# A gated recurrence and a highway layer on one core: a new order of all operations

## The chip, the cores and the metric

The kernel runs on one core of a Trainium2 chip. The metric is the device time of one execution in microseconds (us); lower is better. The engines are named as the profile names them: PE (TensorE matmul), PEld (TensorE weight load), DVE (VectorE), ACT (ScalarE), POOL (GpSimd) and SP (SyncE, which here only issues DMAs).

## What is computed

```python
# x, f_logit: (4, 6336, 256) float32;  lower_bound, b_t: (256);  w_h, w_t: (256, 256)
f = lower_bound + (1 - lower_bound) * sigmoid(f_logit)
for t in range(S):                       # separately for each of the 4 sequences
    h = f[:, t] * h + (1 - f[:, t]) * x[:, t]
    y[:, t] = h
H = relu(y @ w_h)
T = sigmoid(y @ w_t + b_t)
out = T * H + (1 - T) * y
```

The recurrence runs along the sequence, so it is one long chain over 6336 steps for each sequence; the highway layer behind it works on each token alone.

## The kernel before

The 25,344 tokens are cut into 28 units (list `units`, L42 on): two of 256 tokens, one of 512, 23 of 1024, one of 512 and one of 256. A unit holds 2, 4 or 8 blocks of 128 tokens. The 256 channels are two halves `h` of 128, and the recurrence is done with channels on partitions and tokens along the free axis. One tuple of `units` ends with a number, the split: of the product `e = d * t` of that unit, the elements below the split are done by POOL in pieces of 512, and the rest by DVE in one piece.

Every operation of the kernel is a token of one long string, `order`. The loop at the end of the kernel reads the tokens from left to right and calls `do_<letter>` for each; every instruction is pinned to that order on its engine (`pin`). `s12.1:0` is the scan of unit 12, half 1, into buffer 0 of its kind; a `v` behind the numbers puts the operation on DVE instead of its usual engine; `*5` puts five matmuls on zeros ahead of it. Thus the string settles the order on each engine, SP's queue of DMAs among them, and which buffer each tile takes. A tile that takes a buffer waits until the last reader of the tile before it is done.

What the letters do for unit `n`, with the line that the profile shows:

- `l`, `x`: DMA of the logits and of the inputs, 1 MB each for a full unit (L263, issued by SP; six buffers each). `w`: DMA of half an output unit (L394, SP).
- `u`: sigmoid of minus the logits for the whole unit (ACT, L275). `b`: `u * x` for two blocks (POOL, or DVE with `v`, L283).
- `i`: transposes of `u` for one half into PSUM (PE, L289). `f`: the gate of that half from them (ACT L300, or DVE with `v`, L298). `p`: transposes of `b` (PE, L309). `i` and `p` share two PSUM buffers.
- `s`: the scan of one half (DVE, L326).
- `z`, `g`: the two products with the weights (PE, L338 and L141). `t`: sigmoid of `z` (ACT, L351). `d`: the rest of the relu and the difference to y (DVE, L355). `E`, `e`: `d * t` on POOL in pieces, and on DVE (L360).
- `o`: adds `e` and the scaled y and transposes back (PE, L379 and L380). `c`: copy from PSUM (ACT L389, or DVE with `v`, L387). `z`, `g` and `o` share three PSUM buffers.
- Single words: `wh`, `wt` (weight DMAs), `pc`, `cc`, `dg`, `WH`, `WTa` (constants and scaled weights), `k` (matmuls on zeros).

`shared` adds one more dependence: the first POOL operation behind a DVE operation of kind `b`, `e`, `dg` or `WH` in the list waits for that DVE operation.

```python
        if not gpsimd:
            held[:] = [ins]
        elif held:
            tc.add_manual_dep(ins.ins, held.pop().ins.name, mybir.DependencyInfo(
```

Of the kernel before, what the change touches and what calls it, by code (L numbers as in the profile page):

```python
# [83 lines left out]
f7.0:1 c4.1:2 d6.0:0 p7.0:0 E5.0 i8.0:1 z6.1:0 s7.0 u10:1 z6.0:1 g6.1:2 b8.3 l12:5 f8.0:0 b8.1 E5.3 E5.2 w3.1 w4.1
i9.0:1 p8.0:0 b9.3 b9.2 d6.1 o5.1:2 s8.0:0 t6.1:0 t6.0 f9.0:2 g7.0:1 i9.1:1 E6.3:0 c5.1:3 p8.1:0 x10:4 E6.2 z7.0:0
l11:0 E6.1 d7.0:2 o5.0:2 f9.1:1 g7.1:1 u12:0 s8.1 c5.0:0 p9.1:1 d7.1 i10.1:0 t7.0:1 f10.1:0 z8.0:2 z7.1:1 b10.0:1
b10.1 g8.1:0 p9.0:0 t8.0:2 z8.1:2 t7.1 s9.1:2 d8.1:1 u11:2 g8.0:1 w5.1 i12.1:1 E6.0 t8.1 b10.2 s9.0 x11:5 b10.3
f12.1:3 o6.1:0 e7:2 x12:0 d8.0 o6.0:2 i11.1:1 w5.0 p10.1:0 b11.3:2 z9.0:1 c6.1:1 f11.1:1 e8:1 b12.3:0 i10.0:1 g9.0:0
l13:1 c6.0:2 s10.1:1 t9.0:0 b11.1 b11.0 l15:2 b12.0 z9.1:2 f10.0:2 p10.0:0 o7.1:1 w6.1 i11.0:1 t9.1 g9.1:2 c7.1:3
d9.0:0 s10.0 o7.0:1 d9.1 f11.0:0 b11.2 p11.0:0 w6.0 b12.2 u13:1 s11.0:3 E9.1:0 x13:1 z10.1:2 E9.0 c7.0:0 e9 t10.1:1  # L90
g10.1:0 w7.1 i13.1:1 d10.1:2 b12.1 p11.1:0 s11.1 u15:2 g10.0:2 E9.2 o9.1:1 o9.0:0 f13.1:2 x15:2 E8.0 l14:3 b13.0:1
i12.0:1 b13.2 c9.1:1 w7.0 b13.3 i15.1:0 z11.0:1 b15.1:2 f12.0:0 p12.0:1 d10.0 z10.0:2 c9.0:2 x14:3 t11.0:0 o8.0:0
f15.1v:1 t10.0 w9.0 p12.1:0 b13.1 o8.1:2 s12.0:2 g11.1:1 c8.0:3 s12.1 i13.0:1 u14:0 E10.0:2 z12.1:0 b15.0 w9.1 d11.1:0
p13.1:0 z11.1:1 f13.0:0 i14.1:1 c8.1:0 e10 b14.1:0 w8.0 s13.1:0 g11.0:2 b14.2 t12.1:2 t11.1 l16:4 z12.0:0 b14.3
f14.1:3 w8.1 b14.0 x16:4 g12.0:1 t12.0 i14.0:0 p13.0:1 f14.0:2 d11.0 o10.0:2 d12.0:1 o10.1:1 c10.0:2 s13.0 l17:5
g12.1:0 E11.2:0 E11.0 E11.1 i15.0:1 p14.1:0 d12.1 c10.1:1 u16:1 z13.0:2 g13.0:0 e12:1 t13.0:1 f15.0:0 s14.1:1 o11.0:1
c11.0:3 E11.3 z13.1:2 p14.0:1 b16.3:1 b15.2 t13.1 b15.3 i16.0:0 f16.0:3 o11.1:1 d13.0:2 b16.0 g13.1:2 i16.1:0 w10.1
s14.0 c11.1:0 w10.0 p15.1:1 l20:0 d13.1 u17:0 w11.0 x17:5 b16.1 E12.0 s15.1:3 f16.1:2 z14.1:1 z14.0:0 b16.2 g14.1:2
d14.1:0 p15.0:1 l19:1 w11.1 i17.1:0 t14.1:0 E13.2:2 E13.3 s15.0 o12.1:2 E13.1 t14.0 g14.0:0 l18:2 x19:0 x18:1 u20:2
o12.0:1 c12.1:1 w12.1 d14.0 E13.0 p16.0:1 z15.0:2 b17.1:0 l21:3 f17.1:1 b17.0 b17.3 c12.0:2 E14.2:0 p16.1:0 t15.0:2  # L100
b17.2 s16.0:2 o13.1:1 g15.0:0 E14.1 i17.0:1 u19:1 o13.0:2 s16.1 f17.0:0 d15.0:1 p17.0:0 s17.0:0 g16.0:0 c13.0:3
c13.1:0 p17.1:1 u18:0 z15.1:1 E14.0 z16.1:2 E14.3 d16.0:2 i19.1:0 s17.1 g16.1:0 t15.1 w12.0 w13.0 x21:3 g15.1:1 d15.1
f19.1:3 w13.1 i18.0:0 i20.0:1 b19.1:2 b19.3 t16.1:1 g17.0:2 x20:2 b18.2:1 f18.0:2 i18.1:0 o14.0:1 b18.0 d16.1 d17.0:0
b18.3 b18.1 e15:1 E15.1 g17.1:0 o14.1:2 d17.1 b19.2 E15.0 f20.0:0 f18.1:1 c14.0:1 p18.1:1 u21:0 z16.0:1 z17.0:0
s18.1:1 t16.0 p18.0:0 o15.1:1 t17.0:0 b19.0 s18.0 b21.2:0 o15.0:0 c14.1:2 p19.1:1 z17.1:2 c15.1:3 e16:2 E17.1:0
b20.1:1 c15.0:0 i19.0:0 z18.1:1 b20.0 b20.3 l22:4 t17.1 b20.2 w14.0 g18.0:0 f19.0:1 z18.0:2 w14.1 p19.0:0 s19.1:3
E17.3 i20.1:1 d18.0:1 w15.1 t18.1:2 t18.0 o16.1:1 E17.0 g18.1:2 o16.0:0 b21.1 s19.0 d18.1 f20.1:2 w15.0 p20.0:1
i21.1:0 l23:5 u22:1 b21.0 g19.1:2 c16.1:1 s20.0:2 f21.1:3 b21.3 E17.2 c16.0:2 g19.0:1 i21.0:0 d19.1:2 f21.0:1 i22.0:1
z19.1:0 p20.1:0 f22.0:0 o17.1:2 p21.1:1 d19.0 x22:4 z19.0:1 t19.1:1 s20.1 c17.1:3 o17.0:2 w16.1 u23:2 w16.0 l24:0
i23.1:0 E19.2:1 g20.1:0 e18:2 t19.0 z20.1:1 b22.0:2 f23.1:2 p21.0:0 s21.1:0 i22.1:1 c17.0:0 b22.2 E19.0 b22.3 d20.1:0  # L110
b22.1 s21.0 g20.0:0 o18.0:2 t20.1:0 f22.1:3 u24:0 o18.1:1 p22.1:0 p22.0:1 x23:5 w17.1 d20.0 E19.1 z20.0:0 c18.0:1
z21.1:2 c18.1:2 z21.0:1 s22.1:1 t20.0 i24.0:0 w17.0 s22.0 x24:1 E19.3 g21.1:0 b23.2:1 t21.1:2 f24.0:1 b23.3 t21.0
d21.1:1 b23.1 g21.0:2 i24.1:1 d21.0 l25:1 b23.0 w18.0 E21.2:0 f24.1:3 i23.0:0 o19.1:0 e20:2 g22.1:1 o19.0:2 f23.0:0
w18.1 c19.1:3 c19.0:0 b24.0:0 b24.2 x25:0 p23.1:1 b24.1 p23.0:0 z22.1:0 u25:1 d22.1:2 l27:2 o20.0:2 s23.1:3 o20.1:1
c20.0:1 i25.1:1 b24.3 c20.1:2 E21.3 s23.0 t22.1:1 g22.0:2 E21.0 z22.0:1 f25.1:2 b25.1:2 w19.1 b25.2 w19.0 p24.0:0
z23.1:0 b25.0 t22.0 d22.0 l26:3 g23.1:2 t23.1:0 b25.3 i25.0:1 z23.0:1 s24.0:2 w20.0 p24.1:0 f25.0:0 o21.0:0 w20.1
d23.1:0 p25.0:1 g23.0:2 s24.1 u27:2 E21.1 t23.0 g24.1:1 c21.0:3 x26:2 u26:0 o21.1:0 E22.1:1 E22.3 d23.0 E22.0 p25.1:0
x27:3 d24.1:1 o22.1:2 E22.2 b26.1:1 b26.0 z24.1:1 c21.1:0 s25.0:0 c22.1:1 E23.0:2 z24.0:0 o22.0:2 i26.1:1 t24.1:2
# [316 lines left out]
```

## Time and profile before

| what | value |
|---|---|
| time, median of 3 runs (range) | 210.58 us (210.58 to 211.62) |
| the profiled execution: its own time, its span | 210.7 us, 208.9 us |
| DVE busy | 195.6 us, 155 instructions |
| ACT busy | 193.6 us, 189 instructions |
| PE busy | 192.8 us, 1827 instructions |
| POOL busy | 173.4 us, 164 instructions |
| mean DMA rate over the span | 377 GB/s, 78.69 MB moved |
| granted TensorE clock | 0.996 |

The span is the stretch from the first to the last instruction or transfer of the profiled execution; its own time is 1.8 us longer. A busy engine is one with an instruction under way; matmuls overlap, so PE's busy share is not its load. A group's mean is the time of one instruction, and neighbours on one engine overlap by some 0.07 to 0.1 us.

### The profile page before, as it was taken

Reading aid. Unit: us, or ns where it says so; the run is one execution under the profiler, and the core shown is the slowest. Engines: PE = TensorE matmul, PEld = TensorE weight load, DVE = VectorE, ACT = ScalarE, POOL = GpSimd, SP = SyncE. Lnnn points to the kernel's source line nnn. Section 1 sums busy time; section 2 is a strip of 40 time slices with the busy share of each in tenths; the row PEclk is TensorE's granted clock in tenths of the full one; section 3 lists DMA queues with packets and bytes.
Section 4 is the critical chain, followed back from the end, with each engine's and each line's share of the span. In section 5 each row is a group of like instructions: output and inputs, shape, how many; then the busy total and the mean of one; then the engine's idle time right before and its main releaser. Section 6 shows DMA issues by size and latency. Waiting matters only on the chain.

```text
span 208.9 us, 4672 instructions
## 1 busy us (share of the span) xinstructions
PE 192.8 (92%) x1827; PEld 132.9 (64%) x1827; DVE 195.6 (94%) x155; ACT 193.6 (93%) x189; POOL 173.4 (83%) x164
## 2 busy tenths in 40 slices
...
GB/s 226 393 426 417 416 419 425 417 408 424 416 422 405 420 401 346 402 413 378 421 384 381 425 417 420 427 414 427 406 362 315 322 418 409 368 229 190 176 328 254
DMA packets 15982, 78.69 MB, mean 377 GB/s; under 512 B 1748, under 2 KB 2264, under 8 KB 10072
## 3 DMA queue, kind: packets, MB, share of 16 engines
...
q8 instruction: 14, 0.23, 0.4%
q14 instruction: 8, 0.07, 0.1%
q10 hardware_dynamic: 8, 0.00, 0.0%
...
## 4 chain that ended last, share of the span: by engine, by line
PE 44%; DVE 20%; DMA 13%; ACT 10%; issue 6%; POOL 4%; SPq 1%; DVEq 0%; ACTq 0%
DMA l<-in_f_logit_dram 13%; DVE y L326 11%; DVE d L355 7%; PE g L338 6%; PE z L338 6%; PE op L379 6%; PE op L380 6%; PE g L141 5%; PE z L141 5%; PE bT L309 5%; PE uT L289 4%; ACT u L275 3%; ACT f L300 3%; ACT o L389 3%; DVE e L360 2%
## 5 line engine op out<-in xcount | busy, mean ns | idle before, releaser
L283 POOL TENSOR_TENSOR bv<-u,x 128x512 bf16<-128x512 f16 x96 | 110.0, 1183 | 20.9 <-DMA x<-in_x_dram 10.1
L326 DVE TENSOR_TENSOR_SCAN y<-f,y,bT 128x1024 bf16<-128x1024 f16 (+5 forms) x54 | 106.7, 1992 | 1.3 <-ACT f L300 0.6
L360 POOL TENSOR_TENSOR e<-d,t 128x512 bf16<-128x512 bf16 (+1 forms) x57 | 64.4, 1154 | 9.2 <-DVE e L360 5.7
L355 DVE SCALAR_TENSOR_TENSOR d<-y,ncc,g 128x1024 bf16<-128x1024 bf16 (+2 forms) x56 | 63.0, 1141 | 0.8 <-PE g L338 0.5
L300 ACT ACTIVATE f<-uT,ncc 128x1024 f16<-128x1024 f16 (+2 forms) x52 | 55.7, 1090 | 3.5 <-PE uT L289 3.3
L351 ACT ACTIVATE t<-z,bt 128x1024 bf16<-128x1024 f32 (+2 forms) x56 | 57.5, 1063 | 0.7 <-PE z L338 0.4
L389 ACT COPY o<-op 128x1024 f32<-128x1024 f32 (+1 forms) x49 | 49.6, 1042 | 4.1 <-PE op L380 2.9
L379 PE MATMUL op<-diag,y 128*128 128x128 f16 x396 | 49.2, 219 | 2.5 <-ACT t L351 1.3
L275 ACT ACTIVATE u<-l 128x2048 f16<-128x2048 f32 (+2 forms) x28 | 49.1, 1756 | 2.7 <-DMA l<-in_f_logit_dram 2.7
L380 PE MATMUL op<-ident_b,e 128*128 128x128 bf16 x396 | 49.2, 219 | 0.3 <-POOL e L360 0.2
L380 PEld LDWEIGHTS <-e 128*128 128x128 bf16 x396 | 44.0, 113 | 6.6 <-issue 3.1
L379 PEld LDWEIGHTS <-y 128*128 128x128 bf16 x396 | 44.2, 113 | 2.1
L338 PE MATMUL g<-y,w_sb 128*128 128x512 bf16 (+1 forms) x112 | 39.3, 367 | 1.0 <-DVE d L355 0.6
L338 PE MATMUL z<-y,w_sb 128*128 128x512 bf16 (+1 forms) x112 | 39.3, 367 | 0.4 <-DVE d L355 0.4
L309 PE MATMUL bT<-ident_f,bv 128*128 128x128 f32 x198 | 31.4, 278 | 4.3 <-ACT f L300 2.4
L141 PE MATMUL g<-y,w_sb 128*128 128x512 bf16 x92 | 34.9, 379 | 0.0
L141 PE MATMUL z<-y,w_sb 128*128 128x512 bf16 x92 | 34.9, 379 | 0.0
L289 PEld LDWEIGHTS <-u 128*128 128x128 f16 x396 | 26.0, 98 | 11.1 <-issue 3.5
L289 PE MATMUL uT<-ident_h,u 128*128 128x128 f16 x396 | 30.5, 220 | 2.6 <-DVE y L326 1.5
L338 PEld LDWEIGHTS <-w_sb 128*128 128x128 f16 x224 | 21.8, 98 | 16.7 <-issue 0.9
L309 PEld LDWEIGHTS bT<-ident_f,bv 128*128 128x128 f32 x198 | 22.3, 141 | 12.7 <-DVE y L326 3.2
L141 PEld LDWEIGHTS <-w_sb 128*128 128x128 f16 x184 | 18.0, 98 | 17.2 <-issue 2.7
...
## 6 DMA issues: line engine op xcount, KB each, us to landing
...
```

The costliest lines, as they stand in the source:

```text
L141: return pe.add_instruction(mybir.InstMatmult(name=nc.get_next_instruction_name(), start_tensor_calc=start, stop_tensor_calc=stop, tile_si ...
L283: shared(pin(e.tensor_mul(st[n]["bv"][:, k].rearrange("p d j -> p j d"), st[n]["u"][:, q:q + 2], st[n]["x"][:, q:q + 2])), not eng)
L289: pin(nc.tensor.transpose(uT[:, j * P:(j + 1) * P], st[n]["u"][:, j, h * P:(h + 1) * P], ident_h))
L300: pin(nc.scalar.activation(to, of, AF.Identity, scale=ncc[:, h:h + 1], bias=1.0))
L309: pin(nc.tensor.transpose(words[:, k:k + g * (P - 1) + 1:g], pair, ident_f))
L326: pin(nc.vector.tensor_tensor_scan(y[:, c:e], st[n]["f", h][:, c:e], st[n]["bT", h][:, c:e], 0.0 if fresh else carry[h], op0=ALU.mult, op1 ...
L338: pin(nc.tensor.matmul(p[:, a:e], w, half(n, "y", ki)[:, a:e], start=ki == 0, stop=ki == NH - 1))
L351: pin(nc.scalar.activation(half(n, "t", m), st[n]["z", m][:, :tokens(n)], AF.Sigmoid, bias=bt[:, m:m + 1]))
L355: pin(nc.vector.scalar_tensor_tensor(half(n, "d", m), half(n, "y", m), ncc[:, m:m + 1], st[n]["g", m][:, :tokens(n)], op0=ALU.mult, op1=AL ...
L360: shared(pin(eng.tensor_mul(st[n]["e"][:, a:e], st[n]["d"][:, a:e], st[n]["t"][:, a:e])), eng is nc.gpsimd)
L379: pin(nc.tensor.matmul(o, half(n, "y", h)[:, cols], diag[:, h], start=True, stop=False))
L380: pin(nc.tensor.matmul(o, half(n, "e", h)[:, cols], ident_b, start=False, stop=True))
```

## The change

The string `order` is replaced as a whole, and with it the splits in `units`. No function changes, and the units have the same sizes and tokens. By count, of 865 tokens before and 871 after: the DVE pieces of `e` go from 16 to 19, POOL's pieces from 57 to 59 (55 of 512 and two of 256, against 54 and five); DVE's `b` from three to two and POOL's from 96 to 97; DVE's `f` from four to five (four shapes of 256, 256, 512 and 1024 tokens, against five of 256); DVE's two copies `c` are now both of four blocks. The matmuls on zeros that tokens ask for go from 24 to 17. All loads, scans, products and stores are the same in number and size.

The diff, cut to the splits that differ most in the first and last units, and to the beginning and the end of the string:

```diff
     units = [
-        (0, 128, 2, 0, 'y', 4, 512),
+        (0, 128, 2, 0, 'y', 4, 0),
         (0, 128, 2, 256, 'y', 4, 512),
-        (0, 128, 4, 512, 'y', 4, 1024),
-        (0, 128, 8, 1024, 'y', 4, 512),
-        (0, 128, 8, 2048, 'y', 4, 0),
+        (0, 128, 4, 512, 'y', 4, 512),
+        (0, 128, 8, 1024, 'y', 4, 2048),
+        (0, 128, 8, 2048, 'y', 4, 512),
...
-        (0, 128, 4, 24576, 'y', 4, 512),
-        (0, 128, 2, 25088, 'y', 4, 256),
+        (0, 128, 4, 24576, 'y', 4, 0),
+        (0, 128, 2, 25088, 'y', 4, 0),
     ]
     order = """
-l0:0 l3:1 pc:1 wh u0:0 i0.0:1 i0.1:0 k*10 l1:2 x0:0 wt cc dg f0.1v:0 f0.0:1 x1:1 u3:1 u1:2 i1.0*5:0 WH b0.0v:0 l2:3
-x2:2 f1.0:2 p0.1*2:1 b1.0:1 i1.1:0 x3:3 l4:4 s0.1:0 p0.0:1 s0.0 f1.1:3 p1.1*2:0 p1.0:1 g0.0:0 s1.1:1 u2:0 b2.0:2
-i2.1:0 b2.1 s1.0 x4:4 i2.0:1 g0.1:1 g1.0:2 b3.2:0 d0.0:0 g1.1:0 WTa f2.1v:0 i3.1:0 f2.0:1 l5:5 l7:0 d0.1 p2.0*1:1
-z0.1:1 d1.0:1 f3.1:3 z0.0:2 i3.0:0 d1.1 s2.0:2 p2.1:1 t0.1:0 b3.3v x5:5 t0.0 z1.1:0 s2.1 l6:1 g2.0*4:1 b3.1 b3.0v
-f3.0:2 u4:2 x6:0 z1.0:2 E0.0:0 b4.2:1 b4.1 t1.0:1 b4.0 p3.1:0 t1.1 i4.1:1 b4.3 f4.1:1 o0.0:2 g2.1:0 d2.0:2 z2.1:1
-s3.1:3 p3.0:1 c0.0:0 z2.0:2 w0.0 d2.1 t2.1:2 l8:2 i4.0:0 E1.0:1 t2.0 f4.0:0 x7:1 E2.1:2 E2.0 s3.0 p4.1:0 z3.1:1 u5:0
-s4.1:0 p4.0:1 b5.2:2 g3.0:0 t3.1:0 s4.0 b5.1 i5.1:0 d3.0:0 u7:1 g3.1:1 f5.1:3 u6:2 i7.1:1 i5.0:0 g4.1:2 f7.1:2 d3.1
-g4.0:0 o2.0:1 f5.0:1 c2.0:1 d4.1:2 b5.0 b5.3 l9:3 w2.0 p5.0:1 z3.0:2 b6.0:0 b6.3 p5.1:0 b6.2 x8:2 b6.1 t3.0 o1.0:2
...
+l0:0 l3:1 pc:0 u0:0 wh i0.1:0 cc i0.0:1 k*4 u3:1 f0.0v:0 i3.1*6:1 l1:2 x0:0 u1:2 f0.1v:1 l2:3 wt dg x1:1 i1.1:0 k*3
+f3.1:2 WH f1.1v:3 x2:2 b0.0:0 p0.1:0 p0.0:1 s0.1:0 b1.0:1 WTa s0.0 i1.0:0 f1.0v:1 u2:0 z0.0*1:2 x3:3 g0.0:0 d0.0:0
+l4:4 b2.0:2 p1.0*1:1 s1.0:1 t0.0:0 p1.1:0 x4:4 s1.1 g0.1:0 i2.1:1 z0.1:2 d0.1 g1.0:1 i3.0:0 b2.1 f2.1:0 g1.1:0 t0.1
+l5:5 d1.0:1 f3.0:1 z1.0:2 b3.3v:0 z1.1:1 e0:0 b3.1v p2.1:0 t1.0:1 t1.1 i2.0:1 f2.0:3 b3.2 p2.0:1 b3.0 d1.1 s2.1:2
+p3.1*2:0 u4:2 E1.0:1 s2.0 x5:5 i4.1:1 o0.0:2 f4.1:0 g2.0:1 z2.1:0 c0.0:0 s3.1:3 l6:0 w0.0 d2.0:2 i4.0:1 p3.0:0 b4.2:1
+t2.1:2 b4.1 o1.0:1 f4.0:3 z2.0:0 c1.0:1 t2.0 b4.0 b4.3 s3.0 u5:0 g2.1:2 p4.0:1 z3.0:1 s4.0:0 d2.1 i5.0:0 p4.1:1 g3.0:0
+E2.0:2 b5.0:2 t3.0:0 b5.3 f5.0:2 b5.2 u6:1 s4.1 i5.1:0 f5.1:1 g3.1:2 x6:0 i6.0:1 b5.1 z3.1:1 p5.0:0 f6.0:3 i6.1:1 w1.0
+d3.0:0 t3.1 e2 o2.0:0 g4.0:1 l7:1 b6.1:0 b6.3 d3.1 f6.1:0 x7:1 b6.0 b6.2 E3.0:0 c2.0:2 s5.0:1 l8:2 E3.2 z4.1:2 u7:2
...
-o23.1:2 w23.0 b27.0:0 E25.1:1 i27.0:1 w24.0 g26.0:1 c24.1:1 z26.1:0 c23.1:2 e25 p27.0:0 E25.2 f27.0v:0 w23.1 i27.1:1
-d26.0:0 z26.0:2 g26.1:1 s27.0:2 E25.0 d26.1 t26.1:0 t26.0 f27.1:2 E26.0:0 o25.1:0 p27.1:1 s27.1 o25.0:2 z27.0:1 e26
-c25.1:3 t27.0:2 w24.1 c25.0v:0 o26.0:0 g27.0:1 d27.0:1 z27.1:2 g27.1:1 d27.1 c26.0:2 t27.1 E27.0:2 e27 w25.1 w25.0
-o27.0:1 w26.0 c27.0:1 w27.0
...
+g26.1:0 d26.1:0 E24.0 E25.1:1 p27.1:0 s27.1:3 f27.0v:3 o24.1:2 c23.0:3 g26.0:1 w23.1 c24.1:1 o24.0:0 z26.1:2 p27.0:1
+d26.0 w23.0 e25 s27.0 c24.0:2 t26.1:0 E25.0 o25.1:1 z27.0:0 z26.0:2 w24.1 c25.1v:0 t27.0:2 t26.0 E25.2 z27.1:0 w24.0
+t27.1 e26:2 o25.0:1 g27.1:2 c25.0:3 w25.1 o26.0:0 d27.1:2 g27.0:2 d27.0 e27:0 c26.0:1 o27.0:1 w25.0 c27.0:2 w26.0
+w27.0
 """
```

More of the change, by code (lines that the diff above doesn't have):

```diff
@@ L84 @@
[L84 to L118, printed above, removed]
@@ new lines @@
+c6.1:1 s9.1 g9.1:0 i10.0:0 u11:1 d8.1 f10.0:3 z9.1:1 E7.3 c6.0v:2 p10.0:1 t9.1:0 E7.0 i11.0:0 E7.1 d9.1:0 b11.2:2
+o7.0:2 z9.0:0 f11.0:1 s10.0:2 p10.1:0 x12:0 b11.0 w5.1 l13:1 s10.1 o7.1:1 b11.1 c7.0:3 w6.1 g9.0:2 i11.1:1 d9.0 l14:2
+E8.1:2 i12.0:0 t9.0 g10.1:0 b11.3 w6.0 u13:2 x13:1 z10.0:2 b12.0:0 c7.1:0 e9:0 E9.0 f11.1:3 p11.1:1 z10.1:1 d10.1:1
+w7.0 w7.1 x14:2 f12.0:2 i13.1:0 o9.0:0 u14:1 b12.2 t10.0:1 s11.1:3 E8.0 p11.0:1 g10.0:2 c9.0:1 e8 s11.0 t10.1 o9.1:0
+b12.1 f13.1:3 o8.1:1 b12.3 p12.1:1 c9.1:2 i14.0:0 b13.3:1 d10.0 c8.1:3 g11.1:2 z11.0:1 f14.0:1 s12.1:1 b13.0 i13.0:0
@@ new lines @@
+t11.0:0 l15:3 w9.0 b13.1 p12.0:1 e10:1 d11.1:0 E10.1 z11.1:0 g11.0:1 f13.0:0 x15:3 b13.2 w8.1 s12.0 p13.1:0 b14.0:2
+o8.0:2 t11.1 u15:0 z12.0:0 i15.0:1 d11.0 s13.1:0 b14.2 w9.1 E10.0 c8.0:0 z12.1:1 b14.1 E11.2:0 g12.0:2 E11.0 t12.0:2
+o10.0:0 t12.1 l16:5 E11.1 p13.0:0 g12.1:1 d12.0:2 s13.0 b14.3 d12.1 l17:4 w8.0 f15.0:2 c10.0:1 i15.1:1 f15.1:3 o10.1:2
+x16:4 o11.0:0 c10.1:3 w10.0 p14.0:1 b15.3:0 E11.3 c11.0:2 b15.0 s14.0:2 g13.1:2 z13.1:0 i14.1:0 o11.1:1 u16:2 E12.2:2
+f14.1:0 E12.1 p14.1:1 b15.1 d13.1:1 z13.0:2 w10.1 b15.2 c11.1:0 s14.1 t13.1:1 E12.3 E12.0 g13.0:1 g14.1:0 d13.0 u17:1
@@ new lines @@
+w11.0 i16.0:0 l18:0 f16.0:1 b16.3:1 p15.1:1 z14.1:1 i17.1:0 t13.0 b16.0 g14.0:2 d14.1:0 z14.0:0 f17.1:0 b16.2 p15.0:0
+w11.1 t14.1:0 s15.1:3 i17.0:1 x17:5 d14.0 s15.0 t14.0 f17.0:3 o12.1:2 l19:1 b16.1 o12.0:0 c12.1:1 x18:0 l20:2 e13:1
+c12.0:3 e14:0 E13.0 i16.1:1 b17.0:2 g15.0:2 p16.0:0 z15.0:1 f16.1:2 b17.3 E14.0 d15.0:2 p16.1:1 b17.2 u18:0 s16.0:1
+b17.1 o13.0:2 o13.1:0 i18.1:0 t15.0:2 c13.0:2 g15.1:1 u19:2 s16.1 g16.0:2 x19:1 c13.1:0 d15.1 E14.1 w13.0 p17.1:1
+z15.1:1 b18.3:0 f18.1:1 p17.0:0 t15.1 b18.1 b18.0 d16.0:1 z16.1:0 u20:1 s17.1:0 s17.0 b18.2 t16.1:1 o14.1:1 g16.1:2
```

62 lines of the change are left out of this document (41 added, 21 removed).

## The prediction

> **What bounds the kernel now.** I read the page's busy times first, then busy time by stage, then the timelines of DVE, ACT and POOL, the chain of waits, and the end.
>
> ```profile
> PE 192.8 (92%) x1827; PEld 132.9 (64%) x1827; DVE 195.6 (94%) x155; ACT 193.6 (93%) x189; POOL 173.4 (83%) x164
> ```
>
> ```profile
> 0.00:10.00 10.00, 8.74 (x35) 3.74 (x35) 3.81 (x15) 5.56 (x8) 1.74 (x12) 1.00 0.83 306
> 10.00:20.00 10.00, 8.33 (x69) 5.48 (x69) 9.21 (x15) 8.36 (x12) 6.61 (x6) 1.00 1.02 422
> 20.00:40.00 20.00, 15.95 (x138) 10.38 (x136) 19.28 (x12) 18.62 (x18) 18.90 (x18) 1.00 1.01 417
> 120.00:160.00 40.00, 38.49 (x379) 27.20 (x377) 40.00 (x28) 39.99 (x37) 36.58 (x34) 1.00 1.01 403
> 180.00:200.00 20.00, 20.00 (x214) 14.66 (x213) 19.90 (x18) 17.65 (x21) 17.34 (x16) 1.00 0.56 221
> 200.00:209.00 9.00, 4.38 (x57) 3.41 (x54) 3.75 (x7) 3.65 (x6) 1.86 (x3) 0.90 0.74 290
> ```
>
> The columns of the second fence are the stage, its length, then the busy time of PE, PEld, DVE, ACT and POOL, the clock, the share of DMA and GB/s. From 20 us to 200 us DVE is idle for about a microsecond in all; ACT is full too, and DMA moves some 400 GB/s until 160 us. So DVE's chain is the time: 195.6 us of work, 7.0 us idle in the first 20 us, 0.7 us up to 40 us, about 0.4 us up to 200 us, and the end. A new list can only win where DVE stands still, and it loses wherever it makes DVE wait.
>
> Where DVE and ACT wait after the start, the timelines and the chain say:
>
> ```profile
> 31.13 1.92 ACT L275 ACTIVATE u<-l 128x2048 f16<-128x2048 f32 x1 [1.01 <-DMA l<-in_f_logit_dram]
> 35.09 4.58 DVE L326 TENSOR_TENSOR_SCAN y<-f,y,bT 128x1024 bf16<-128x1024 f16 x2 [0.58 <-ACT f L300]
> ```
>
> ```profile
> 11.05 19.98 DMA l<-in_f_logit_dram
> ```
>
> This is `u6`: its logits were issued at 11.05 us and landed at 31.03 us, behind everything issued before. ACT lost 1.01 us, and the scan of unit 5 lost 0.58 us on DVE. The end is short:
>
> ```profile
> 204.42 0.29 DVE L360 TENSOR_TENSOR e<-d,t 128x256 bf16<-128x256 bf16 x1
> 205.26 0.59 ACT L389 COPY o<-op 128x512 f32<-128x512 f32 x1 [1.16 <-PE op L380]
> ```
>
> From the last `e` it is 4.2 us to the span's end: 16 op matmuls, a copy, and 3.05 us for the last store.
>
> **The change, part by part.** The sum goes against the profiled execution: 208.9 us of span in 210.7 us of time, 0.12 us above the median of 210.58.
>
> *Work.* By means of the groups (2048: 1225 ns, 1792: 1092, 1536: 988, 1024: 726, 512: 471, 256: 291; by line between neighbours 1280: 857, 768: 599), DVE's `e` was 14.33 us in 16 pieces and becomes 14.94 us in 19 (three each of 2048, 1536, 1280 and 1024, five of 512, two of 768): +0.62. DVE's `f` was 1270 + 745 + 2 x 476 = 2.97 us and becomes 5 x 476 = 2.38: -0.59. Its copies were 1217 + 666 and become 2 x 1217: +0.55. One `b` less: -0.73. DVE in all: **-0.15 us**. ACT: `f` gains one of 1171 and one of 698 and loses three of 472 (+0.45), the copies lose one of 1062 and gain one of 582 (-0.48): -0.03. POOL: one `b` more and 54 + 5 `E` for 55 + 2 (1183 - 1171 + 3 x 684): +2.1 us, to 175.5 of a span with 35 us idle; that cover holds it. Seven matmuls on zeros fewer, at 0.22 us start to start, lie in the first 17 us where PE waits for data; if PE were late there they would be a gain of up to 1.5 us of PE.
>
> *The beginning.* I followed the new list by hand with durations and landing times of this trace. POOL now does `b0.0` (0.73 us on DVE, 1.18 on POOL), so `s0.1` moves from 9.7 to about 10.0 us; `p1.0` and `i2.1` share a PSUM buffer, and so do `f2.0`'s tile and `p2.0`. `s3.1` starts near 19.6 us (19.79 before) with 0.33 us less work done on DVE: +0.1 us. Then the loads: before, 10.5 MiB are issued up to and with `l6`, since `l7` is ahead of it; now it is 9.5 MiB. At 31.03 us for 10.5 MiB and 418 GB/s (2.5 us per MiB), `l6` lands near 28.4 us. ACT reaches `u6` near 28.3 us: its wait of 1.01 us is gone. What is late next is POOL: `b3.2` now waits for DVE's `b3.1` (end near 16.8 us), then `b3.2`, `b3.0`, `E1.0` and four `b4` at 1.14 us each bring `p4.0` to 25.2 us, where `s4.0` could begin at 24.75: 0.5 us of DVE. The scan of unit 5 begins near 33.2 us with 1.6 us less work done by DVE, so equal to 34.8 against 35.09 us before: **-0.3 us**, the first +0.1 in it. Ends: -0.8 us if POOL is in time, +0.5 us if the walk missed a wait as long as the one at 35.09 us and the gain is lost as well. I take -0.3, which is what the walk gave.
>
> SP's queue: `w0.0` and `w1.0` stand ahead of `l7`, `x6` and `x7`, which were ahead of `w0.0` before or had more time. By my walk `l7` lands near 34.7 us and is wanted near 35.2; `l8` at 39.7 us, wanted at 40.1. It holds by half a microsecond.
>
> *The middle.* DVE's and ACT's work, summed along each list, cross closest at `d22.0` before (0.7 us) and at `s23.0` now (1.0 us): 0.3 us tighter. ACT gains some 0.7 us at `u6` against DVE's 0.3, which pays for that: **0**, between 0 and 1.5 us (the longest wait of a PE transpose for ACT's `f` is 1.4 us).
>
> *Instruction packets of PE.* The page counts 14 packets of 0.23 MB on the instruction queue. Idle time of PEld put down to issue reaches 1.08 us at 37.0 us, yet DVE works through it; from 40 us on DVE has 0.4 us to win. So this costs and brings nothing by itself.
>
> *The end.* From `s24.1` DVE has 22.1 us left (22.7 before), ACT 18.0 (19.9), POOL 16.4 (17.5). By hand: last scan done at 19.45 us from there, `e26` at 21.65, `d27.0` at 23.7, `e27` at 24.1, `c27` at 25.25, and 3.05 us for the store: 28.3 us, against 208.9 - 180.5 = 28.4 before. **-0.1 us**, between -0.5 (the lead of ACT and POOL is of use) and +1.0 (`g27.0` waits for `d27.1` behind `o26.0`, and a slip there counts in full).
>
> Sum: -0.15 - 0.3 + 0 - 0.1 = -0.55, so 210.7 - 0.55 = **210.1 us**. About 0.5% (1.05 us) is what a measurement of this kernel can tell from no change, and this lies within it.
>
> **The rivals.** *DVE and POOL meet (slower).* A DVE `e` that comes while POOL is in the middle of an operation is held up for the rest of it. The rows:
>
> ```profile
> 192.03 1.17 POOL L360 TENSOR_TENSOR e<-d,t 128x512 bf16<-128x512 bf16 x1 [1.52 <-DVE e L360]
> 192.97 0.77 DVE L360 TENSOR_TENSOR e<-d,t 128x1024 bf16<-128x1024 bf16 x1
> 132.65 0.68 DVE L360 TENSOR_TENSOR e<-d,t 128x1024 bf16<-128x1024 bf16 x1
> ```
>
> The `e` at 192.97 us met POOL for its last 0.23 us and took 0.77 us; the one at 132.65 us met a POOL that had just ended and took 0.68. In the timelines no DVE `e` overlaps POOL by more than 0.3 us: the list before brings each to the end of a POOL piece. The new list has 19 `e` and two `b` on DVE, at other places. If DVE and POOL drift apart by half a piece (0.58 us) where these meet, five hits cost 5 x 0.58 = 2.9 us of a full DVE: 213.0 us. It decides once two hits come (+1.2 us). For it: POOL has 2.1 us more and three more pieces meet. Against it: each following POOL piece waits for the `e`, which lines them up again, and in my walk `e0`, `e2` and `e4` find POOL at rest. [...] The trace shows only overlaps of up to 0.3 us, with 0.1 us lost at 192.97, so a full block is not seen here.
>
> *The loads come late (slower).* If `c1.0` is a microsecond late, `w1.0` holds `l7` in SP's queue, `u7` waits, and the half microsecond in hand turns into a wait of 1 us as at 31 us before, again at `u8`: +1.0 for the two, and the 0.3 us gain gone: 211.4 to 212. For it: DMA is full there. Against it: the loads wanted later are further ahead in the new list by 1 to 2 us.
>
> *Both ends win (faster).* `s4.0` does not wait (-0.8 at the beginning) and the end takes its -0.5: 210.7 - 0.15 - 0.8 - 0.5 = 209.2 us. For it: less work left from `s24.1` on every engine but PE. Against it: the chain in the end runs through buffers, not work.
>
> **How the numbers follow.** Forecast 0.37 (its own range 209.5 to 211.3), both ends win 0.33, the port 0.20, the loads 0.10. That is faster by over 0.5% 0.33, within it 0.37, slower 0.30. The low end takes the faster case with the 0.7 us below it that a middle without its own small waits and a head as early would add (208.5); the high end stops at 213.0, the price of five hits.
>
> **What would show it.** Right: `u6` without a wait for its DMA, DVE busy between 195 and 196 us, DVE idle by 40 us near 7.4 (7.7 before), and 28 to 29 us from `s24.1` to the end. [...] The loads: ACT's `u` waiting over 2.7 us for DMA in all. Wrong altogether: DVE idle over 1.5 us between 40 and 200 us, or ACT or PE as its releaser there.

## The result and the profile after

The new list is slower: 211.73 us, median of 14 runs (211.28 to 213.5), against 210.63 us for the list before, median of 14 (210.56 to 211.62). The ratio is 1.006, with an interval of 1.0043 to 1.0077: about half a percent, small but clear of the spread. The forecast was 210.1 us.

The profiled execution of the new list took 213.04 us, with a span of 211.2 us, so it lies 1.3 us above the median. The executions fall into two groups, by the clock of TensorE that each one lists. With `again` and `no_store` below (the same list, in `no_store` without one store) there are 24 executions. Nine of them have a mean clock of 0.990 to 0.991 and take 212.02 to 213.04 us, with a median of 212.56. Fourteen have 0.995 or more and take 211.28 to 211.96 us, with a median of 211.52. One, of 213.5 us at a clock of 0.999, fits neither group and stays unexplained. The profile below is one of the nine; `again` is one of the fourteen, so both are shown.

The page of the new list, and busy time by stage (columns as before):

```profile
PE 193.8 (92%) x1820; PEld 132.7 (63%) x1820; DVE 195.2 (92%) x158; ACT 193.3 (92%) x188; POOL 175.2 (83%) x167
```

```profile
0.00:10.00 10.00, 8.36 (x37) 3.52 (x37) 3.64 (x15) 5.58 (x6) 2.77 (x12) 1.00 0.83 304
10.00:20.00 10.00, 6.93 (x50) 4.28 (x50) 8.80 (x14) 7.65 (x12) 6.46 (x6) 0.98 1.03 422
20.00:40.00 20.00, 18.16 (x150) 11.74 (x148) 18.52 (x12) 18.01 (x18) 16.58 (x16) 0.92 1.01 419
120.00:160.00 40.00, 38.04 (x373) 26.75 (x372) 39.83 (x27) 39.64 (x37) 36.93 (x34) 1.00 1.00 384
180.00:200.00 20.00, 19.99 (x212) 14.44 (x211) 19.84 (x17) 17.64 (x20) 19.49 (x19) 1.00 0.55 213
200.00:211.00 11.00, 6.07 (x76) 4.66 (x73) 4.95 (x8) 5.87 (x9) 2.61 (x3) 0.99 0.75 295
```

DVE's work is as forecast, 195.2 us. Its idle time is not: 1.48 us between 20 and 40 us (0.72 before), where the clock column falls to 0.92, and 6.25 us from 200 us to the end (5.15 before).

The wait for the logits of unit 6 is gone: the timeline of ACT in `again` has that `u` without any idle time before it.

```profile
28.59 1.91 ACT L275 ACTIVATE u<-l 128x2048 f16<-128x2048 f32 x1
```

The end, from the timelines of DVE and ACT of the new list:

```profile
206.25 0.42 DVE L360 TENSOR_TENSOR e<-d,t 128x512 bf16<-128x512 bf16 x1
207.38 0.58 ACT L389 COPY o<-op 128x512 f32<-128x512 f32 x1 [0.88 <-PE op L380]
```

From the last `e` it is 4.5 us to the span's end, and from the last copy 3.2 us; these were 4.2 and 3.05 us.

### The profile page after: what moved, and what is told of

It reads as the page before. It is cut to its first block, busy times and chain, and to the rows that moved or that the text cites. A ratio compares the mean times of both kernels' runs of the same rounds, so it can differ in the third digit from the quotient of the medians.

```text
span 211.2 us, 4663 instructions
## 1 busy us (share of the span) xinstructions
PE 193.8 (92%) x1820; PEld 132.7 (63%) x1820; DVE 195.2 (92%) x158; ACT 193.3 (92%) x188; POOL 175.2 (83%) x167
## 4 chain that ended last, share of the span: by engine, by line
PE 52%; DVE 23%; POOL 11%; issue 5%; DMA 3%; ACT 2%; SPq 1%; DVEq 0%; POOLq 0%; ACTq 0%
DVE y L326 16%; PE op L380 8%; PE op L379 7%; PE bT L309 7%; PE g L338 7%; POOL bv L283 7%; PE uT L289 6%; PE z L338 6%; PE z L141 5%; PE g L141 5%; DVE d L355 4%; POOL e L360 4%; DMA x<-in_x_dram 3%; DVE e L360 2%; ACT f L300 2%
## 5 line engine op out<-in xcount | busy, mean ns | idle before, releaser
L283 POOL TENSOR_TENSOR bv<-u,x 128x512 bf16<-128x512 f16 x97 | 111.2, 1175 | 18.1 <-DMA x<-in_x_dram 7.9
L360 POOL TENSOR_TENSOR e<-d,t 128x512 bf16<-128x512 bf16 (+1 forms) x59 | 65.1, 1121 | 9.3 <-DVE e L360 5.3
L351 ACT ACTIVATE t<-z,bt 128x1024 bf16<-128x1024 f32 (+2 forms) x56 | 56.9, 1044 | 2.2 <-PE z L141 1.3
L389 ACT COPY o<-op 128x1024 f32<-128x1024 f32 (+1 forms) x49 | 48.8, 1023 | 2.5 <-PE op L380 1.2
L338 PE MATMUL g<-y,w_sb 128*128 128x512 bf16 (+1 forms) x112 | 40.1, 372 | 1.3 <-DVE y L326 0.9
L309 PE MATMUL bT<-ident_f,bv 128*128 128x128 f32 x198 | 32.1, 280 | 4.8 <-POOL bv L283 1.7
L289 PEld LDWEIGHTS <-u 128*128 128x128 f16 x396 | 26.5, 99 | 13.0 <-issue 3.7
L289 PE MATMUL uT<-ident_h,u 128*128 128x128 f16 x396 | 31.5, 222 | 2.4 <-DVE y L326 1.5
L309 PEld LDWEIGHTS bT<-ident_f,bv 128*128 128x128 f32 x198 | 22.1, 141 | 13.7 <-POOL bv L283 4.6
```

Of the source, the lines that this page charges most:

```text
L283: shared(pin(e.tensor_mul(st[n]["bv"][:, k].rearrange("p d j -> p j d"), st[n]["u"][:, q:q + 2], st[n]["x"][:, q:q + 2])), not eng)
L289: pin(nc.tensor.transpose(uT[:, j * P:(j + 1) * P], st[n]["u"][:, j, h * P:(h + 1) * P], ident_h))
L309: pin(nc.tensor.transpose(words[:, k:k + g * (P - 1) + 1:g], pair, ident_f))
L338: pin(nc.tensor.matmul(p[:, a:e], w, half(n, "y", ki)[:, a:e], start=ki == 0, stop=ki == NH - 1))
L351: pin(nc.scalar.activation(half(n, "t", m), st[n]["z", m][:, :tokens(n)], AF.Sigmoid, bias=bt[:, m:m + 1]))
L360: shared(pin(eng.tensor_mul(st[n]["e"][:, a:e], st[n]["d"][:, a:e], st[n]["t"][:, a:e])), eng is nc.gpsimd)
```

## The experiments

### The new list again

The same kernel, with no edit.

> The new list unchanged. Clock theory: PE's granted clock halves for some 3 us at about 20 us in a part of the executions only (mean clock 0.990 to 0.992 there, 0.995 or more elsewhere); executions with it take 212.0 to 213.1 us, those without 211.3 to 211.9. If this profile shows no drop, DVE's idle time up to 40 us is 8 us or less (9.0 in the first profile). Rival, that the waits at 20 to 25 us come from POOL's b and the shared PSUM buffers: the three waits of the scan of unit 3, d of unit 2 and the scan of unit 4 (0.68, 0.21, 0.75 us) are there in every profile.

It took 212.07 us (211.39 to 212.85, 6 runs), ratio 1.0067 with an interval of 1.0048 to 1.0085. Its profiled execution had no drop of the clock, with 211.39 us and a span of 209.6 us, so it is the one to hold against the 208.9 us before. The time up to the scan `s24.1`, and from there to the end, by the view of stages for DVE alone (stage, length, busy time with instructions, clock, share of DMA, GB/s), for the list before and then for `again`:

```profile
0.00:180.51 180.51, 172.49 (x133) 1.00 1.00 398
180.51:208.90 28.39, 23.14 (x24) 0.97 0.61 241
```

```profile
0.00:180.95 180.95, 172.58 (x136) 1.00 1.00 397
180.95:209.60 28.65, 22.46 (x23) 0.98 0.60 236
```

Length less busy time is DVE's idle time. In all, the new list has 0.59 us less work on DVE (0.09 more ahead of `s24.1`, 0.68 less behind it) and 1.29 us more waiting (0.35 ahead, 8.37 for 8.02; 0.94 behind, 6.19 for 5.25). So without the clock it loses 0.70 us, and most of the new waiting lies in the last 29 us. This execution is one of the shorter ones of its group, whose median lies 0.9 us above the list before; what adds the last 0.2 us is not known. DVE's idle time up to 40 us is 7.83 us, as the clock theory said, and of the rival's three waits only that of the scan of unit 3 is left, at 0.42 us.

### The clock at 20 us: warm and cold

In the profiled execution of the new list PE's clock halves near 20 us. The view of stages in steps of 2 us, for the new list and then for `again`:

```profile
16.00:18.00 2.00, 0.86 (x8) 0.71 (x9) 2.00 (x4) 1.91 (x5) 1.01 (x1) 1.00 1.02 422
18.00:20.00 2.00, 1.48 (x8) 0.78 (x7) 1.59 (x2) 1.52 (x1) 2.00 (x3) 0.90 1.00 414
20.00:22.00 2.00, 2.00 (x19) 1.86 (x17) 1.72 (x1) 0.82 (x1) 2.00 (x3) 0.50 1.01 418
22.00:24.00 2.00, 2.00 (x15) 1.17 (x14) 1.37 (x2) 1.33 (x3) 2.00 (x3) 0.75 1.02 418
```

```profile
18.00:20.00 2.00, 1.27 (x13) 0.97 (x13) 1.56 (x3) 1.32 (x1) 2.00 (x2) 1.00 1.06 438
20.00:22.00 2.00, 2.00 (x24) 1.33 (x21) 2.00 (x1) 1.69 (x3) 2.00 (x3) 1.00 0.99 410
```

In steps of 0.2 us the same view of the new list gives a clock of 1.00 up to 19.6 us, 0.50 in every step from there to 23.0 us, 0.96 in the step behind and 1.00 again from 23.2 us: 3.4 us at half speed, and the means 0.90, 0.50 and 0.75 add up to the same (0.4 + 2.0 + 1.0). DVE waits for PE three times there, in its timeline of the new list:

```profile
20.28 2.35 DVE L326 TENSOR_TENSOR_SCAN y<-f,y,bT 128x1024 bf16<-128x1024 f16 x1 [0.68 <-PE bT L309]
22.84 0.75 DVE L355 SCALAR_TENSOR_TENSOR d<-y,ncc,g 128x512 bf16<-128x512 bf16 x1 [0.21 <-PE g L338]
24.33 4.83 DVE L326 TENSOR_TENSOR_SCAN y<-f,y,bT 128x1024 bf16<-128x1024 f16 x2 [0.75 <-PE bT L309]
```

`s4.0` starts at 24.33 us here and at 22.91 us in `again`: 1.4 us, of which some 0.2 were there before the drop. Eight transposes of that stretch, those of `i4.1`, take 1.06 us at half clock and 0.61 at full. The two experiments on it change only matmuls on zeros. `warm` adds eight of them to the new list, between 15 and 21 us; `cold` takes nine off the list before, ahead of 18 us.

```diff
 (warm, on the new list)
-z1.1:1 ... p2.0:1 ... p3.1*2:0 ... i4.1:1
+z1.1*3:1 ... p2.0*1:1 ... p3.1*4:0 ... i4.1*2:1
 (cold, on the list before)
-p0.1*2:1 ... p1.1*2:0 ... p2.0*1:1 ... g2.0*4:1
+p0.1:1 ... p1.1:0 ... p2.0:1 ... g2.0:1
```

> The new list with eight more matmuls on zeros between 15 and 21 us (z1.1, p2.0, p3.1, i4.1), in places where PE waits. Clock theory: clock 1.00 in each 2 us stage up to 40 us, the time 211.3 to 211.6 us with no execution above 212. Rival (POOL and PSUM buffers make the waits): the waits at the scans of units 3 and 4 stay, and the time is 211.7 to 212.

> The list before without the nine matmuls on zeros of p0.1, p1.1, p2.0 and g2.0 (9.9 to 18 us). Clock theory: the clock halves at about 20 us in some executions, the median rises by 0.3 to 1.5 us and the spread over 1 us. Rival (zeros do not matter): 210.6 us, spread below 0.3 us.

`warm` took 211.68 us (211.46 to 212.07, 5 runs), ratio 1.0047 (1.0035 to 1.0059). None of its five executions has a clock below 0.994, and neither has any of the five of `end_warm` below, with the same zeros; if nine in 24 were still the rule, ten in a row without a drop would come about once in a hundred times. The time misses the expected range by 0.1 us and one execution lies above 212 us, and the scans of units 3 and 4 still wait 0.28 and 0.20 us in its profile: the rival, POOL and the PSUM buffers, has a small part. `warm` stays about 1 us above the list before, so the clock is not the whole loss.

`cold` took 210.83 us (210.51 to 211.09, 11 runs), ratio 1.0007 (0.9998 to 1.0015), which is not clear of no change. Both of its expectations missed: the clock drops, but earlier, to a mean of 0.66 from 10 to 20 us in the profiled execution, and ten of the eleven executions have a mean clock below 0.99. DVE does lose by it at first: `s3.1` starts at 20.91 us, 1.1 us later than in the list before. But in the list before ACT waits at 31 us for the logits of unit 6 in any case (1.01 us, the row in the prediction). In `cold` it comes to the same `u6` late and without a wait (lines numbered one higher):

```profile
31.14 1.91 ACT L276 ACTIVATE u<-l 128x2048 f16<-128x2048 f32 x1
```

So half of the delay ends there: the scan of unit 5 starts 0.55 us later than before (35.64 us), and `s24.1` only 0.12 us; where the rest went was not traced. The new list has lost that wait, which was its gain, and with it a place that takes up a delay: `s4.0` is 1.4 us later with the drop than in `again`, and so is `s24.1` (182.34 us for 180.95). The drop between 19.6 and 23 us costs about 1 us by the medians of the two groups (212.56 for 211.52 us). The fewer zeros count by where they leave PE slow: between 10 and 18 us in `cold`, at a ratio of 1.0007 in all, and from 19.6 to 23 us in the new list.

Of the nine executions only one was traced; `tail_old`, whose beginning is that of the new list, has a mean clock of 0.990 and shows the drop in the same place (0.99 up to 20 us, 0.72 from 20 to 25 us). For the others the mean clock is all there is. In the trace of the new list with the drop the longest idle time of PE between 14 and 20 us is 0.78 us. `again` has the same gap and only a little more work there (1.06 of 2 us from 16 to 18 us, 0.86 in the trace with the drop) and no drop. So thin work is not enough by itself, and what decides between two executions was not tested.

### Splices in the head and the middle

To place the loss, lists were put together from both. `head_new` is the new order up to 38 us and the old one behind it, `head_old` the reverse; `mid_new` has only the middle new. `tail_new` and `tail_old` change over near 160 us. Buffers and splits follow the list that an operation comes from.

```diff
 (head_new, on the list before: the first 168 tokens of the new list, then the rest in the old order)
-l0:0 l3:1 pc:1 wh u0:0 i0.0:1
+l0:0 l3:1 pc:0 u0:0 wh i0.1:0
...
+d4.1 E3.3 g5.1:2 d5.1:2
 (tail_new, on the list before: 691 tokens kept, then the rest in the new order)
-o27.0:1 w26.0 c27.0:1 w27.0
+o27.0:1 w25.0 c27.0:2 w26.0 w27.0
```

> The new list up to its 168th token (about 38 us), then everything left in the order of the list before. If the beginning alone carries the loss (clock, and waits at 20 to 25 us): 211.0 to 212, with the spread of the new list. If the beginning is as forecast, 0.3 us better, and the loss lies behind it: 210.3 to 210.6 without a clock drop.

> The list before up to its 169th token (about 38 us), then everything left in the order of the new list. If the beginning carries the loss: 210.4 to 210.7 us with a spread below 0.3 us. If middle and end carry it: 211.2 to 211.6, and little spread, since no clock drop is to be had at 20 us.

> The list before up to about 38 us, the new list's middle from there to about 160 us, the end of the list before. If the middle costs 0.2 to 0.3 us as DVE's idle time between 40 and 180 us says: 210.8 to 210.9. If it costs nothing, 210.6; if it carries the loss in executions without a clock drop, 211.3.

`head_new` took 216.83 us (1.0297), `head_old` 214.67 (1.0194) and `mid_new` 215.15 (1.021). All three are slower than both lists. DVE is idle for 6.0, 1.5 and 1.5 us between 40 and 80 us, where each list by itself has 0.2 us: the seam costs more than what was to be found. The expected times were 210.3 to 212 us, so all three missed. They say nothing of where the loss lies.

> The list before up to about 160 us (691 tokens), then the new list's order. If the end costs 0.5 us as the two profiles say (28.9 us from the scan of unit 24, half 1, to the span's end against 28.4): 211.0 to 211.2. If the end is as forecast (28.3): 210.5.

> The new list up to about 160 us (695 tokens), then the order of the list before. End theory: 0.5 us below the new list, 210.8 to 211.0 without a clock drop, 211.5 to 212.5 with it. If the end is worth nothing: as the new list, 211.3 to 211.9 and up.

`tail_new` took 211.97 us (211.66 to 213.11, 6 runs), ratio 1.0072 (1.0054 to 1.009). Its head is that of the list before (DVE idle for 6.99 us up to 20 us, before 6.98), yet its span is 209.9 us, and DVE is idle for 6.09 us from 200 us on, as in `again` (6.0). `tail_old` took 211.99 us (211.74 to 213.19, 6 runs), ratio 1.0075 (1.0057 to 1.0093). Its idle time at the end is back at 5.35 us, but the splice puts 0.7 us more work on DVE than the list before (some 196.3 us in all), and its profiled execution has the drop of the clock. Both times miss what the end theory gave, and that of `tail_old` is what was expected if the end were worth nothing.

Part of what a seam adds can be read off: DVE and POOL meet. The rows of `tail_new`, then of `tail_old`, lines numbered one higher:

```profile
166.43 3.42 POOL L284 TENSOR_TENSOR bv<-u,x 128x512 bf16<-128x512 f16 x3
168.68 2.25 DVE L361 TENSOR_TENSOR e<-d,t 128x2048 bf16<-128x2048 bf16 x1
```

```profile
170.34 1.16 POOL L361 TENSOR_TENSOR e<-d,t 128x512 bf16<-128x512 bf16 x1 [1.47 <-ACT t L352]
170.90 1.69 DVE L361 TENSOR_TENSOR e<-d,t 128x2048 bf16<-128x2048 bf16 x1
```

An `e` of 2048 elements takes 1.23 us in the list before. Where POOL is busy for the first 1.17 us of it, it takes 2.25 us; where POOL is busy for the first 0.60 us, 1.69 us. So DVE loses most of the time for which the two meet, about 1.0 and 0.5 us here, the latter a good part of the 0.7 us more work in `tail_old`. In `mid_new` one takes 1.70 us in the same way, and in `head_new` one takes 2.14 us and the POOL piece beside it 2.15 us instead of 1.17. That is the mechanism of the forecast's first rival, and it is part of the seam's price; the rest was not traced.

In `tail_new` and `tail_old` these meetings lie ahead of `s24.1`. From `s24.1` to the span's end it is 28.39 us in the list before, 28.37 in `cold` and 28.43 in `tail_old`; in the new order it is 28.65 in `again`, 28.60 in `warm`, 28.76 in `tail_new` and 28.86 in the first profile. So the end of the new order is 0.2 to 0.5 us longer, whatever stands ahead of it and with or without the drop. That is a part of the loss and not the whole of it.

### The end by itself

The waits that the forecast had named are there. DVE's and ACT's timelines of `again`, from 200 us (here the last scan, `s27.0`, ends at 200.3 us):

```profile
200.59 1.23 DVE L387 COPY o<-op 128x1024 f32<-128x1024 f32 x1 [0.29 <-PE op L380]
202.06 0.69 DVE L360 TENSOR_TENSOR e<-d,t 128x1024 bf16<-128x1024 bf16 x1 [0.24 <-ACT t L351]
203.25 0.48 DVE L355 SCALAR_TENSOR_TENSOR d<-y,ncc,g 128x256 bf16<-128x256 bf16 x1 [0.50 <-PE g L338]
204.29 0.48 DVE L355 SCALAR_TENSOR_TENSOR d<-y,ncc,g 128x256 bf16<-128x256 bf16 x1 [0.56 <-PE g L338]
204.88 0.42 DVE L360 TENSOR_TENSOR e<-d,t 128x512 bf16<-128x512 bf16 x1
```

```profile
203.00 2.12 ACT L389 COPY o<-op 128x1024 f32<-128x1024 f32 x2 [0.61 <-ACT t L351]
206.00 0.59 ACT L389 COPY o<-op 128x512 f32<-128x512 f32 x1 [0.88 <-PE op L380]
```

The four waits are 1.59 us. In the list before, DVE waits once behind its last scan, 0.47 us at `d27.1`:

```profile
203.84 0.48 DVE L355 SCALAR_TENSOR_TENSOR d<-y,ncc,g 128x256 bf16<-128x256 bf16 x1 [0.47 <-PE g L338]
```

`end_new` takes the two waits of `d27.1` and `d27.0` away by order and buffers; `end_warm` does the same on `warm`; `end_old` uses the same rule on the list before.

```diff
 (end_new, on the new list)
-e26:2 o25.0:1 g27.1:2 c25.0:3 w25.1 o26.0:0 d27.1:2 g27.0:2 d27.0 e27:0 c26.0:1 o27.0:1 w25.0 c27.0:2
+e26:2 g27.1:2 g27.0:0 o25.0:1 d27.1:2 c25.0:3 w25.1 o26.0:2 d27.0 e27:0 c26.0:1 o27.0:0 w25.0 c27.0v:2
 (end_old, on the list before)
-e26 c25.1:3 t27.0:2 w24.1 c25.0v:0 o26.0:0 g27.0:1 d27.0:1 z27.1:2 g27.1:1 d27.1 c26.0:2 t27.1 E27.0:2 e27
+e26 c25.1:3 t27.0:2 w24.1 z27.1:0 c25.0v:0 g27.0:1 t27.1 d27.0:1 g27.1:0 d27.1 o26.0:2 E27.0:2 e27
-w25.1 w25.0 o27.0:1 w26.0 c27.0:1 w27.0
+w25.1 w25.0 c26.0:2 o27.0:1 w26.0 c27.0v:1 w27.0
```

> The changed list with only its last 16 tokens put in another order: `g27.1` and `g27.0` go ahead of `o25.0` and take two buffers of their own (2, behind `t26.0`, and 0, behind `t27.1`), so that `d27.1` and `d27.0` follow `e26` on DVE at once; `o26.0` takes buffer 2 behind `d27.1`, `o27.0` buffer 0 behind `d27.0`, and the copy of unit 27 is done on DVE. Theory (the added time of the new list lies in its end, in the two waits of 0.50 and 0.56 us of `d27.1` and `d27.0` for their `g`, behind the products of `o25.0` and `o26.0`): the waits go, the last `e` ends about 1.0 us earlier, DVE idle from 200 us to the end falls from 6.0 to 5.0 us or less, span 208.6 to 209.0 without a clock drop against 209.6, median 211.0 (210.7 to 211.3). Rival (the end is set by the last stores, or by PE's products `o`, which still run one after the other): the last `e` comes earlier but the span stays within 0.3 us of 209.6, median 211.6 to 212.0.

> The same new end on the list that has the eight more matmuls on zeros of `warm`, which took away the drop of the PE clock at 20 us. Theory (the change's added time is the end plus, in about a third of the executions, the clock drop): both are gone, no execution above 211.6; median 210.9 (210.6 to 211.2), within 0.2% of the list before. Rival (the middle of the new list costs it, not the end): median at or above 211.5.

> The list before with only its last 19 tokens put in another order, by the same rule: `g27.1` no longer takes the buffer that `d27.0` reads, and `g27.0` runs ahead of `o26.0`; the copy of unit 27 is done on DVE. Its only wait there was 0.47 us of `d27.1`. Theory (such a wait at the end counts in full): the last copy ends about 0.5 us earlier, median 210.1 to 210.4, a kernel that is faster than both. Rival (the last store of the four blocks of unit 26, issued later by this order, sets the end): 210.6 to 211.2.

All three theories missed. `end_new` took 213.28 us (212.35 to 213.42, 5 runs), 1.0129 (1.0113 to 1.0144), three of the five with the drop of the clock and the profiled one, of 212.35 us, without; `end_warm` 212.3 (212.23 to 212.35), 1.0078 (1.0065 to 1.009), all without it; `end_old` 211.81 (211.74 to 211.9), 1.0055 (1.0042 to 1.0068). Yet the edit did what it was made for. DVE's and ACT's timelines of `end_new`, whose lines are numbered one higher:

```profile
202.88 0.87 DVE L356 SCALAR_TENSOR_TENSOR d<-y,ncc,g 128x256 bf16<-128x256 bf16 x2
203.85 0.43 DVE L361 TENSOR_TENSOR e<-d,t 128x512 bf16<-128x512 bf16 x1
```

```profile
204.01 1.93 ACT L390 COPY o<-op 128x1024 f32<-128x1024 f32 x2 [1.40 <-issue]
```

Both `d` run without a wait and the last `e` ends at 204.28 us instead of 205.30. But `g27.1` and `g27.0` now stand ahead of `o25.0` and `o26.0` on PE, and ACT's two copies of four blocks start at 204.01 us instead of 203.00. Behind the first of them come the last 1.28 MB of stores. What the DMA engines move between 199 and 212 us, in slices of 0.325 us, for `again` and then for `end_new`:

```profile
GB/s 403 252 378 441 378 315 391 416 403 366 25 315 429 403 403 88 50 25 391 403 403 416 403 416 416 378 353 397 82 0 0 0 0 0 0 0 0 0 0 0
```

```profile
GB/s 416 403 202 429 378 378 391 366 416 403 227 88 403 416 403 328 25 38 50 0 0 353 416 391 416 403 416 391 403 334 397 114 0 0 0 0 0 0 0 0
```

The last stretch of about ten full slices (3.3 us at 400 GB/s is 1.3 MB) has no gap in it: it ends near 208.2 us in `again` and 209.2 us in `end_new`, each 1.4 us ahead of the span's end. So the stores are what `end_new` seems to wait for. Counting a copy as 1.02 us, `c25.0` ends at 204.02 us in `again` and at 205.03 in `end_new`, and both spans end 5.6 us later.

### Moving the last 15 us alone, and one store fewer

`end_swap2` is the list before up to `s26.1` (195 us) and the new order behind it, `end_swap` the reverse. `no_store` and `end_no_store` leave out the store of blocks 0 to 3 of unit 25, in the new list and in `end_new`.

```diff
 (end_swap2: the list before up to here, then the rest in the new order)
 w22.1 e24 g25.0:2 o24.0:1 w22.0 s26.1:1
-c23.0:3 E24.1 c24.0:0 o24.1:0 d25.0 s26.0
+b27.0:0 d25.0:1 i27.1:1 o23.1:2 E24.1 f27.1:1 s26.0:2
...
 (no_store, on the new list; end_no_store likewise on end_new)
-o27.0:1 w25.0 c27.0:2 w26.0 w27.0
+o27.0:1 c27.0:2 w26.0 w27.0
```

> The list before up to and with `s26.1` (about 195 us), then the rest in the new order with the new splits of units 26 and 27 only. Theory (the new end is the cost): the beginning and the middle are those of before, so the idle time of DVE from 200 us to the end is near 6.0 us against 5.15, and the median is 211.3 to 211.8. Rival (the added time lies in the beginning and the middle of the new list): within 0.3 us of 210.66.

> The new list up to and with `s26.1`, then the rest in the order before, with the splits of units 26 and 27 of before only; POOL again does half of unit 26. Theory: DVE idle from 200 us to the end returns to 5.2 to 5.4 us, and executions without a clock drop at 20 us come to 210.5 to 211.0. Rival: 211.3 or more without a clock drop.

`end_swap2` took 215.61 us (1.0232) and `end_swap` 221.14 us (1.0496). The seam again: in `end_swap` DVE waits 3.84 us for a `g` and 4.60 us for a transpose behind it. Both miss what was expected, and neither tells the two causes apart.

> The changed list without the store `w25.0` (512 KB, the third from last; four blocks of unit 25 stay unwritten). Two chains end at the span's end of 209.6 us in `again`: the copy `c27.0` that ends at 206.59, with 3.05 us from there to the end (as in the list before: 205.85 to 208.9), behind the waits of `d27.1` and `d27.0`; and the last 1.28 MB of stores that wait for `c25.0`, which ends at 204.05, with 5.55 us to the end. If the copy of unit 27 sets the end, nothing changes: span 209.6 without a clock drop. If the stores alone set it, the span falls to 208.8 to 209.2.

> `end_new` without the same store. There the last `e` ended 1.0 us earlier than in `again`, yet the span was 1.0 us longer, with `c25.0` ending 0.93 us later and 5.62 us from there to the end. Theory (the stores behind `c25.0` set the end of `end_new`): the span falls from 210.6 to 209.3 to 209.8, since 768 KB instead of 1.28 MB are left to stream. Rival (something else there, the order of the copies on ACT): it stays within 0.3 us of 210.6.

`no_store` took 211.91 us (211.42 to 212.56, 4 runs). Its profiled execution, at a clock of 0.997, has the same span of 209.6 us with 512 KB less to write. So the store `w25.0` does not set the end of the new list by itself: the copy of unit 27, which ends at 206.62 us here, 3.0 us ahead of the span's end, holds the same end. That is the chain behind the waits of DVE. `end_no_store` took 211.96 us (211.72 to 212.24, 4 runs), with a span of 210.1 us for 210.6. 0.15 us of that were there at `s24.1` already (181.04 us for 181.19), so the store was part of what held `end_new`, by some 0.35 us and not by the 0.8 or more expected. In it the next store waits for `c26.0`, which ends at 205.81 us, 4.3 us ahead of the end.

Put together, three chains end within about a quarter of a microsecond of each other in `again`: from `c27.0` 206.59 + 3.05 = 209.64, from `c25.0` 204.02 + 5.57 = 209.59, from `c26.0` 205.12 + 4.3 = 209.4. The offsets are those of the list before, of `end_new` and of `end_no_store`. In the list before they come to 205.85 + 3.05 = 208.9, 202.79 + 5.57 = 208.4 and 203.72 + 4.3 = 208.0. The first chain is 0.74 us later in the new list, as much as the difference of the two spans; by this sum one chain cannot be shortened there without the next one holding the end. `end_old` does not fit: 205.28 + 3.05 and 204.90 + 4.3 give 208.3 and 209.2, and its span is 210.1 us. In its trace a trickle of 27 GB/s, a fifteenth of the full rate, runs on to 208.7 us. Why is open. No version that was tried beats the list before.

## Why the prediction was wrong, step by step

The sign was wrong: it was -0.55 us against the profiled execution, and `again` is +0.70 us by span, with the drop of the clock on top in nine of 24 executions.

| step | forecast, us | measured in `again`, us |
|---|---|---|
| DVE's work in all | -0.15 | -0.59 |
| of it ahead of `s24.1` | not split off | +0.09 |
| DVE's idle time to 40 us | -0.3 | +0.13 (7.83 for 7.70) |
| DVE's idle time from 40 us to `s24.1` | 0 | +0.22 (0.54 for 0.32) |
| from `s24.1` to the span's end | -0.1 | +0.26 (28.65 for 28.39) |

*The sum.* The four measured parts +0.09, +0.13, +0.22 and +0.26 make the +0.70. The forecast's own terms were not such parts. Its -0.1 for the end ran from `s24.1` to the span's end and so held the 0.6 us less of work there (22.1 for 22.7), while the -0.15 for work in all held the same 0.6 us once more. With -0.15 in all and -0.6 of it behind `s24.1`, the work ahead is +0.45, and the terms as they stood give +0.45 - 0.3 + 0 - 0.1 = +0.05, that is 210.75 us. This step failed first: the double count is 0.6 us of the error of 1.25 us. The rest is 0.43 at the beginning, 0.22 in the middle and 0.36 at the end, less 0.36 for the work ahead of `s24.1`, which came to +0.09 and not +0.45. So even with the sum put right, the terms for the three stretches were too low by 1.01 us together.

*The end* was mis-sized. The forecast had -0.1 with a bound of +1.0 for a slip of `g27.0` behind `d27.1` and `o26.0`. The walk by hand slipped by little at each point: from `s24.1`, `e26` is done at 21.80 us (21.65 by the walk), `d27.0` at 23.82 (23.7), `e27` at 24.35 (24.1), `c27` at 25.64 (25.25) and the span at 28.65 (28.3). That is 0.36 us. DVE's idle time behind `s24.1` grew by 0.94 us and ate the 0.68 us of work that the list had moved away from there.

*The beginning* was mis-sized too. `u6` does not wait, as forecast, and the scan of unit 5 starts at 33.45 us in `again`, 33.2 by the walk. The gain at 35 us is real: DVE is idle for 0.35 us from 20 to 40 us instead of 0.72. But the first 20 us cost 0.49 us (7.47 for 6.98) where the walk had +0.1: `s3.1` starts at 19.82 us, not 19.6, and waits 0.42 us for the transposes of `p3.1`, which wait for POOL's `b3.0`:

```profile
19.82 2.35 DVE L326 TENSOR_TENSOR_SCAN y<-f,y,bT 128x1024 bf16<-128x1024 f16 x1 [0.42 <-PE bT L309]
```

The half microsecond of `s4.0` that the walk had charged did not come without the drop of the clock.

*The middle* had been put at 0 and cost 0.22 us. The longest single gap there, 0.2 us, stands ahead of a `d` near 147 us, and the profile names nothing that DVE waited for; why is open. No experiment separates this part or that of the beginning.

*The zeros.* The step "if PE were late there they would be a gain of up to 1.5 us of PE" looked only at PE's time. What fewer zeros can take away is the clock, 3.4 us at half speed where DVE has no slack: with eight more, none of ten executions had the drop. This was in no rival.

*DVE's work* came out 0.44 us lower than the -0.15. By the means of `again` the 19 pieces of `e` make 14.65 us where 14.94 had been used, for instance 444 ns for 512 elements instead of 471 and 940 for 1536 instead of 988: 0.29 us. The rest is not split further; three more instructions on DVE, each overlapping its neighbour by some 0.07 to 0.1 us, could be most of it.

*The rivals.* The meeting of DVE and POOL, called the port in the chances, did not come in the new list: DVE's `e` of 1024 elements takes 749 ns (726 before), every mean lies within 0.05 us of the ones used, and DVE's busy time is 195 us; the longest meeting in `again` is 0.33 us, at 51.52 us. The prediction had seen no full block, with 0.1 us lost of a meeting of 0.23; the rows of `tail_new` and `tail_old` come close to one, with 1.02 us lost of 1.17 and 0.46 of 0.60. So the 0.58 us for a hit of half a piece was an estimate; the meeting of 0.60 us cost 0.46. The loads did not come late: ACT's waits of `u` for DMA are 2.9 us in the profiled execution, above the bound of 2.7 that the forecast had set, but they are those of `u0` and `u3`, both before 7 us, and no later `u` waits. Both ends did not win.

*PE's instruction packets* show no cost that stands out: DVE's idle time from 40 to 200 us is 0.7 us in `again`, below the 1.5 that would have made the forecast wrong altogether.
